# Operand spread with one transfer for both heads, and raw sums stored over 128 partitions, in attention with two dense layers

## Chip, cores and metric

One core of a Trainium2 chip. The metric is the device time of one execution in microseconds, the median of several runs. In the rows below PE is TensorE's matmul and PEld its weight load, DVE is VectorE, ACT is ScalarE, POOL is GpSimd, SP is SyncE; SPq is SyncE's queue, which issues nearly all DMA transfers of this kernel. "L537" is line 537 of the kernel before.

## What is computed

Attention with rotary positions for 4 batches of 8 heads (576 rows of 64), then two dense layers over the 2304 rows: one with a squared ReLU (512 to 2048 to 512), one with a gated SiLU (512 to 1536 to 512). All in float32.

```python
q_rot, k_rot = (rotate(q), rotate(k))
scores = scale * np.matmul(q_rot, k_rot.transpose(0, 1, 3, 2))
scores = scores - np.max(scores, axis=-1, keepdims=True)
attn = np.exp(scores)
attn = attn / (np.sum(attn, axis=-1, keepdims=True) + 1e-09)
attn_out = np.matmul(attn, v)
x = attn_out.transpose(0, 2, 1, 3).reshape(B * S, H * D)
r = np.maximum(x @ w_in, 0.0)
x = (s * (r * r) + b) @ w_out
g = x @ w_gate
out = (g * (1.0 / (1.0 + np.exp(-g))) * (x @ w_val)) @ w_out2
```

## The kernel before

Each float32 operand of a matmul is split into a high and a low part of the type that TensorE reads fast, and products are sums over the parts. The attention goes by pairs of heads, 16 pairs (NP). `prep(p)` loads q and k of a pair (L381), rotates them on GpSimd, transposes them on TensorE (L504) so that q stands in partitions 0 to 63 and k in 64 to 127, and splits the result: ScalarE writes the high part `hi` (tile `qkhi`, L513), VectorE the low part `lo` (`qklo`, L515), each 128 partitions by two heads of S = 576 columns. Both tiles have one buffer.

For pairs 2 to 15, ten transfers on SyncE's queue (L537, called a train in the prediction) then spread these parts over the operand tiles of the score matmuls: `a` (q: high part in the upper 64 partitions, low part in the lower, with 64 zero columns between the heads), `t` (k: low part above, high part below) and `kz` (k's high part above, zeros below). Each transfer has 64 partitions and one head. For pairs 0 and 1 the engines write the operands themselves (L523, L526). The operand tiles exist twice (z = p % 2), so the transfers of pair p overwrite what the scores of pair p - 2 read, and `hi` may be rewritten for pair p + 1 only when the transfers of pair p have read it.

`pair(p)` computes nine blocks of scores (L609), their maxima on VectorE (L612), the exponentials on ScalarE (L616), transposes them (L670, L673), splits them (L678, L685) and multiplies by v (L700, L702). The unnormalized sums of a pair go through `xr` (two buffers) to DRAM tiles `x_d`: for each head one store of the high half's sums (64 partitions) and one of the low half's (L721), so four stores a pair.

The dense layers run over five blocks of 512 or 384 rows. `x_load` brings a block from `x_d`, one transfer for each half (`xl`, `xh`) and batch piece, over 128 partitions (L750); GpSimd adds the halves (L778) and multiplies by reciprocals read from `r_d` (L766, L781), and the result is split. Block 0's load and conversion fall into the attention; each later block is loaded while the block before it is computed. The second layer reads its blocks from `y_d` by the same function.

The order of instructions on each engine is written out by a planner (`Schedule`): every operation has a priority and a reckoned duration, a transfer 0.55 us of SyncE, `size / 360e3` us of the DMA engines and 1.3 us to land. An engine runs its queue strictly in the written order, whatever is late. SyncE's queue also carries v (L433 to L437), q and k, the weights (L287, L289), `r_d` and the outputs. Transfers use eight completion slots in turn.

The lines of the spread and of the store:

```python
for s0, s1, d0 in a_pieces(0, 2 * S):
    n = s1 - s0
    ops.append(sp(a[0:64, d0:d0 + n], lambda s0=s0, s1=s1: st["hi"][0:64, s0:s1], s0 == 0))
    ops.append(sp(a[64:128, d0:d0 + n], lambda s0=s0, s1=s1: st["lo"][0:64, s0:s1]))
for s0 in (0, S):
    c = slice(s0, s0 + S)
    ops.append(sp(t[64:128, c], lambda c=c: st["hi"][64:128, c]))
    ops.append(sp(t[0:64, c], lambda c=c: st["lo"][64:128, c]))
    ops.append(sp(kz[0:64, c], lambda c=c: st["hi"][64:128, c]))
```

Of the kernel before, what the change touches and what calls it, by code (L numbers as in the profile page):

```python
# [8 lines left out]
F32 = mybir.dt.float32  # L9
F32R = mybir.dt.float32r  # L10
# [167 lines left out]
def tile_attention_moe_moe(  # L178
# [16 lines left out]
    nc = tc.nc  # L195
    B, H, S, D = q.shape
    NT, DM = out.shape
    KD = DM // 128
    F1 = w_in.shape[1] // 128
    F2 = w_gate.shape[1] // 128  # L200
    HS = S // 2
    NH = B * H
    NP = NH // 2
# [7 lines left out]
    LATE, LAST = 1 << 20, 1 << 21  # L211
# [5 lines left out]
    AVP = 30  # L217
# [4 lines left out]
    sch = Schedule()  # L222
# [7 lines left out]
    dram = ctx.enter_context(tc.tile_pool(name="dram", bufs=1, space=DRAM))  # L230
# [3 lines left out]
    late = {}  # L234
# [12 lines left out]
    at_c = att.enter_context(tc.tile_pool(name="at_c", bufs=1))  # L247
# [7 lines left out]

    x_d = [[dram.tile([DM, S], F32, name=f"x_d{half}{b}") for b in range(B)] for half in range(2)]
    r_d = [dram.tile([H // 2, 2 * S], F32, name=f"r_d{b}") for b in range(B)]
# [7 lines left out]
    a_t = [at_c.tile([128, 2 * S + 128], F32R, name=f"a{z}") for z in range(2)]  # L265
    t_t = [at_c.tile([128, 2 * S], F32R, name=f"t{z}") for z in range(2)]
    kz_t = [at_c.tile([128, 2 * S], F32R, name=f"kz{z}") for z in range(2)]

# [82 lines left out]
    up, dn = slice(0, 64), slice(64, 128)  # L351
# [3 lines left out]

    def a_pieces(c0, c1):

        if c0 < S:
            yield c0, min(c1, S), c0
        if c1 > S:  # L360
            yield max(c0, S), c1, max(c0, S) + 64

    def place(x, g, gap=0):

        c = S // G
        return x.rearrange("p (h s) -> p h s", h=2)[:, :, g * c:(g + 1) * c]
# [46 lines left out]
    def prep(p):  # L413
# [120 lines left out]
        if p > 1:  # L534
            def sp(o, i, first=False):
                return sch.dma(
                    256 * o.shape[1], lambda: nc.sync.dma_start(out=o.bitcast(F32), in_=i().bitcast(F32)), pr + 6, (*trs, *zeros[z]),  # L537
                    (tok,) if first else (), (hi_tok,), pace=1.3
                )
            ops = []  # L540
            for s0, s1, d0 in a_pieces(0, 2 * S):
                n = s1 - s0
                ops.append(sp(a[0:64, d0:d0 + n], lambda s0=s0, s1=s1: st["hi"][0:64, s0:s1], s0 == 0))
                ops.append(sp(a[64:128, d0:d0 + n], lambda s0=s0, s1=s1: st["lo"][0:64, s0:s1]))
            for s0 in (0, S):
                c = slice(s0, s0 + S)
                ops.append(sp(t[64:128, c], lambda c=c: st["hi"][64:128, c]))
                ops.append(sp(t[0:64, c], lambda c=c: st["lo"][64:128, c]))
                ops.append(sp(kz[0:64, c], lambda c=c: st["hi"][64:128, c]))
            for o in ops[1:]:  # L550
                ops[0].next.append(o)
                o.need += 1
# [24 lines left out]
    def pair(p, st):  # L577
# [10 lines left out]
        for u in range(NU):  # L588
# [3 lines left out]
            if u < QA:  # L592
                terms = ((128 * u, 0),)
            elif u == QA:
                terms = ((128 * u, 0), (128 * u + 64, S))
            else:
                terms = ((128 * u + 64, S),)

# [55 lines left out]
        def third(y, pr):  # L654
# [63 lines left out]
            j = y - 1  # L718
            for half in range(2):
                def put(half=half):  # L720
                    nc.sync.dma_start(out=x_d[half][b][128 * pp + 64 * j:128 * pp + 64 * j + 64], in_=st["xr"][64 * half:64 * half + 64, S * j:S * j + S])  # L721
                x_store[b].append(sch.dma(147456, put, pr + 25 + AVP, evs, (), (xr_tok,), pace=1.2))

# [15 lines left out]
    def x_load(st, pieces, n, prio, deps, pool_name, pool, batches=None):  # L739
# [4 lines left out]
        for z, (o, m, src) in enumerate(pieces):  # L744
            def ld(z=z, o=o, m=m, src=src):
                if z == 0:
                    st["xh"] = pool().tile([128, KD, 512], F32R, tag="xh", name="xh")[:, :, 0:n]
                    st["xl"] = pool().tile([128, KD, 512], F32R, tag="xl", name="xl")[:, :, 0:n]
                for name, part in zip(("xl", "xh"), src):
                    nc.sync.dma_start(out=st[name][:, :, o:o + m].bitcast(F32), in_=part.rearrange("(k p) t -> p k t", p=128))  # L750
            lds.append(sch.dma(len(src) * 2048 * m, ld, prio, deps, (xh_tok,) if z == 0 else (), after=lds[-1:]))
            lds[-1].dur = 0.55 * len(src)
# [164 lines left out]
    def block_b(i, j):  # L917
# [4 lines left out]
        for o, m, b, s in x_pieces(sum(UBS[:j]), UB, S):  # L922
            pieces.append((o, m, (x_d[0][b][:, s:s + m], x_d[1][b][:, s:s + m])))
            batches.append((b, s, m, o))
            deps += x_store[b]
# [31 lines left out]
    def block_2(i, j):  # L957
        st = {}
        UB = UBS[j]
        prio = LAST + 2000 * i  # L960
        outs, xh_tok = x_load(st, [(0, UB, (y_d[j],))], UB, prio - 1500 if i else LATE + 1000 * n_b, y_op[j], ("xhb", "xhc"), lambda: late[st["xh_tok"].pool])
        nt = UB // 128
# [64 lines left out]
        for c in range(nt):  # L1027
# [8 lines left out]
            for z in range(2):  # L1036
                b, g = divmod((sum(UBS[:j]) + c * 128) // 64 + z, PC)
                last = i == len(blocks) - 1 and z == 1
                def put(c=c, z=z, b=b, g=g, e=nc.scalar if last else nc.sync):
                    e.dma_start(out=out[b * S:(b + 1) * S].rearrange("(r g) m -> r g m", g=PC)[:, g], in_=st["y", c][64 * z:64 * z + 64])  # L1040
# [49 lines left out]
```

## Time and profile before

| | us |
|---|---|
| median of the runs shown | 1174.75 |
| lowest, highest of the runs | 1172.81, 3986.44 |
| profiled execution: time | 1175.48 |
| profiled execution: span | 1173.7 |

The span goes from the first to the last instruction of the profiled execution; the time of the same execution has 1.8 us more around it. Busy times are shares of the span; a matmul's end is modelled, so instructions of TensorE overlap in the rows, and a busy TensorE is not one at its peak. "PEclk" is the granted clock in parts of full speed. "DMA share" is the busy share of the 16 DMA engines, each packet counted for its whole time, so that it can pass 1. In a timeline the bracket behind an instruction gives the idle time of its engine before it and what ended it; a wait for several things is put down to the one that came last.

### The profile page before, as it was taken

What the parts mean: (1) busy time and instruction counts of PE and PEld (TensorE: products, weight loads), DVE (VectorE), ACT (ScalarE), POOL (GpSimd) and SP (SyncE); (2) the same over time, 40 slices, a digit from 0 to 9 for tenths busy, and PEclk for the clock granted to TensorE, in tenths of its full rate; (3) what the DMA queues carried; (4) which work ended last, traced back from release to release, by engine and by line L of the source; (5) the groups of instructions that cost most, each with busy time, mean ns of one, the idle gap of its engine ahead of it and who ended that gap; (6) DMA issues with size and microseconds to landing.
All of it is one profiled execution on the core that took longest, in us unless ns stands there. A gap on an engine that the chain in (4) does not pass through costs nothing.

```text
span 1173.7 us, 16604 instructions
## 1 busy us (share of the span) xinstructions
PE 1143.1 (97%) x6242; PEld 1009.1 (86%) x6242; DVE 616.2 (52%) x969; ACT 551.5 (47%) x1112; POOL 263.6 (22%) x222
## 2 busy tenths in 40 slices
PE   8989899999999999999999999999999999999998
PEld 7889888898887888888899998888888888899997
DVE  5879788999979943232242798811211211211111
ACT  4879888899877832232232566412111211211211
POOL 6776685743222031020020112200000000000000
PEclk8899999999999999999999999999999999999999
DMA  4588888767375640110110446301100200200100
GB/s 112 117 191 189 228 208 190 201 158 183 94 226 177 216 149 17 56 57 5 64 49 6 135 146 218 112 1 47 25 1 1 63 1 1 63 1 1 27 1 27
DMA packets 126335, 110.39 MB, mean 94 GB/s; under 512 B 68256, under 2 KB 103216, under 8 KB 126256
## 3 DMA queue, kind: packets, MB, share of 16 engines
q1 hardware_dynamic: 126016, 108.95, 34.3%
q8 instruction: 49, 0.80, 0.3%
q10 hardware_dynamic: 240, 0.39, 0.1%
q14 instruction: 30, 0.25, 0.1%
HBM read 69.71 MB, written 18.95 MB: 76 GB/s over the span
## 4 chain that ended last, share of the span: by engine, by line
PE 79%; DVE 8%; ACT 4%; DMA 3%; SPq 2%; issue 2%; POOL 1%; ACTq 0%; POOLq 0%; DVEq 0%
PE hb L798 14%; PE hb L800 14%; PE hb L799 14%; PE acc L799 5%; PE acc L800 5%; PE acc L798 5%; PE acc L983 4%; PE acc L985 4%; PE acc L984 4%; PE ps_s L609 3%; PE ps_t L670 2%; DVE nm L612 2%; SPq L537 2%; DVE pl L685 2%; PE ps_av L700 1%
## 5 line engine op out<-in xcount | busy, mean ns | idle before, releaser
L798 PE MATMUL hb<-xh,w 128*128 128x512 f32 (+1 forms) x800 | 296.3, 370 | 1.9 <-ACT w L331 1.4
L800 PE MATMUL hb<-xh,w 128*128 128x512 f32 (+1 forms) x800 | 296.0, 370 | 0.0
L799 PE MATMUL hb<-xl,w 128*128 128x512 f32 (+1 forms) x800 | 295.6, 370 | 0.0
L1013 DVE TENSOR_TENSOR si<-hb,si 128x512 f32<-128x512 f32 (+1 forms) x60 | 38.3, 638 | 276.4 <-PE hb L800 273.3
L798 PEld LDWEIGHTS hb<-xh,w 128*128 128x128 f32 x800 | 150.2, 188 | 23.8 <-ACT w L331 1.8
L800 PEld LDWEIGHTS hb<-xh,w 128*128 128x128 f32 x800 | 150.1, 188 | 21.0 <-DVE w L338 0.4
L799 PEld LDWEIGHTS hb<-xl,w 128*128 128x128 f32 x800 | 150.1, 188 | 21.0
L799 PE MATMUL acc<-gl,w 128*128 128x512 f32 (+1 forms) x320 | 118.2, 369 | 0.1
L1011 ACT ACTIVATE si<-hb 128x512 f32<-128x512 f32 (+1 forms) x60 | 33.3, 555 | 180.0 <-PE hb L800 174.3
L798 PE MATMUL acc<-gh,w 128*128 128x512 f32 (+1 forms) x320 | 117.9, 368 | 0.0
L800 PE MATMUL acc<-gh,w 128*128 128x512 f32 (+1 forms) x320 | 117.7, 368 | 0.0
L612 DVE TENSOR_REDUCE nm<-ps_s 128x1 f32<-128x576 f32 x144 | 108.3, 752 | 11.7 <-PE ps_s L609 10.4
L609 PE MATMUL ps_s<-t,a 128*128 128x288 f32 x320 | 103.6, 339 | 9.1 <-ACT e L616 7.4
L616 ACT ACTIVATE e<-ps_s,nm 128x576 f32<-128x576 f32 x144 | 107.1, 744 | 8.3 <-DVE nm L612 7.5
L678 ACT ACTIVATE ph<-ps_t 128x512 fp32r<-128x512 f32 x192 | 105.8, 570 | 9.6 <-PE ps_t L670 7.8
L1015 ACT ACTIVATE gh<-si 128x512 fp32r<-128x512 f32 (+1 forms) x60 | 35.4, 589 | 146.2 <-DVE si L1013 146.2
L850 DVE SCALAR_TENSOR_TENSOR r<-r,sv 128x512 f32<-128x512 f32 (+1 forms) x64 | 46.2, 722 | 108.0 <-ACT r L844 108.0
L700 PE MATMUL ps_av<-ph,vh 128*128 128x384 f32 (+1 forms) x320 | 97.8, 326 | 0.4 <-ACT xr L713 0.4
L844 ACT ACTIVATE r<-hb 128x512 f32<-128x512 f32 (+1 forms) x80 | 44.0, 551 | 114.9 <-PE hb L800 103.6
L685 DVE TENSOR_TENSOR pl<-ps_t,ph 128x512 fp32r<-128x512 f32 x144 | 96.0, 684 | 1.8 <-ACT ph L678 0.6
L670 PE MATMUL ps_t<-ident,e 128*128 128x128 f32 x576 | 88.4, 281 | 6.9 <-DVE qklo L515 4.3
L609 PE MATMUL ps_s<-kz,a 128*128 128x288 f32 x320 | 92.8, 305 | 0.1
(80 smaller groups left out, 1962.4 us busy)
## 6 DMA issues: line engine op xcount, KB each, us to landing
raw<-in_moe_w_out_dram SPq DMA_DIRECT2D x28, 512.0 KB, 3.6
x_d<-xr SPq DMA_DIRECT2D x64, 144.0 KB, 2.6
raw<-in_moe_w_in_dram SPq DMA_DIRECT2D x16, 512.0 KB, 3.9
raw<-in_moe_w_gate_dram SPq DMA_DIRECT2D x12, 512.0 KB, 3.5
raw<-in_moe_w_val_dram SPq DMA_DIRECT2D x12, 512.0 KB, 3.7
x<-in_q_dram SPq DMA_DIRECT2D x15, 288.0 KB, 3.6
x<-in_k_dram SPq DMA_DIRECT2D x15, 288.0 KB, 5.0
out_dram<-o SPq DMA_DIRECT2D x33, 128.0 KB, 2.4
```

Of the source, the lines that this page charges most:

```text
L609: nc.tensor.matmul(ps[:, hf * 512:hf * 512 + HS], a[:, q0:q0 + 128], m[:, k0:k0 + HS], start=y == 0, stop=y == len(todo) - 1)
L612: nc.vector.tensor_reduce(out=st["nm"][:, u:u + 1], in_=st["s", u], axis=AX.XY, op=ALU.max, negate=True)
L616: nc.scalar.activation(out=st["e", u].rearrange("p (f n) -> p f n", f=2), in_=st["s", u], func=AF.Exp, bias=st["nm"][:, u:u + 1], accum_ou ...
L670: nc.tensor.transpose(ps[:, z * 128:z * 128 + 128], st["e", u][:, kc * 128:kc * 128 + 128], ident)
L678: nc.scalar.activation(out=st["ph", y][0:rows, 512 * i:512 * i + n], in_=st["pt", y, i][0:rows, 0:n], func=AF.Copy)
L685: nc.vector.tensor_tensor(out=dst, in0=st["pt", y, i][0:rows, 0:n], in1=st["ph", y][0:rows, c].bitcast(F32), op=ALU.subtract)
L700: nc.tensor.matmul(ps, vv, st["ph", y][:, c], start=kc == 0, stop=kc == 4)
L798: nc.tensor.matmul(o, lh, rh, start=first, stop=False)
L799: nc.tensor.matmul(o, lh, rl, start=False, stop=False)
L800: nc.tensor.matmul(o, ll, rh, start=False, stop=last)
L983: nc.tensor.matmul(o, uh[:, cs], w[:, 0], start=first, stop=False)
L984: nc.tensor.matmul(o, uh[:, cs], w[:, 1], start=False, stop=False)
```

## The change

The tiles `t` and `kz` get 8 unused columns after each head (KS = S + 8), so that both heads of a destination can be addressed as one block with a gap, as in `a`. The ten transfers of a pair become five, each with both heads and twice the bytes. The two DRAM tiles of a batch for the halves become one, in which the two halves of a head stand one after the other, so that one store takes all 128 partitions. The load of a block has to gather the rows again: four transfers of 64 partitions for each piece instead of two of 128. The second head's scores read `t` and `kz` from column KS on.

```diff
--- before.py
+++ after.py
@@ -199,6 +199,7 @@
     F1 = w_in.shape[1] // 128
     F2 = w_gate.shape[1] // 128
     HS = S // 2
+    KS = S + 8
     NH = B * H
     NP = NH // 2
     PC = 2 * S // 128
@@ -253,7 +254,7 @@
     pl_p = att.enter_context(tc.tile_pool(name="pl", bufs=2))
     e_p = att.enter_context(tc.tile_pool(name="e", bufs=NE))
 
-    x_d = [[dram.tile([DM, S], F32, name=f"x_d{half}{b}") for b in range(B)] for half in range(2)]
+    x_d = [dram.tile([2 * DM, S], F32, name=f"x_d{b}") for b in range(B)]
     r_d = [dram.tile([H // 2, 2 * S], F32, name=f"r_d{b}") for b in range(B)]
     y_d = [dram.tile([DM, n], F32, name=f"y_d{j}") for j, n in enumerate(UBS)]
 
@@ -263,8 +264,8 @@
     rt = at_c.tile([128, PC, 3, D // 2], F32, name="rt")
     qs_t = at_c.tile([128, 1], F32, name="qs")
     a_t = [at_c.tile([128, 2 * S + 128], F32R, name=f"a{z}") for z in range(2)]
-    t_t = [at_c.tile([128, 2 * S], F32R, name=f"t{z}") for z in range(2)]
-    kz_t = [at_c.tile([128, 2 * S], F32R, name=f"kz{z}") for z in range(2)]
+    t_t = [at_c.tile([128, 2 * KS], F32R, name=f"t{z}") for z in range(2)]
+    kz_t = [at_c.tile([128, 2 * KS], F32R, name=f"kz{z}") for z in range(2)]
 
     def dma(o, i, size, prio, after=()):
         return sch.dma(size, lambda: nc.sync.dma_start(out=o, in_=i), prio, after=after)
@@ -353,14 +354,7 @@
     x_store = {b: [] for b in range(B)}
     spread_op = {}
 
-    def a_pieces(c0, c1):
-
-        if c0 < S:
-            yield c0, min(c1, S), c0
-        if c1 > S:
-            yield max(c0, S), c1, max(c0, S) + 64
-
-    def place(x, g, gap=0):
+    def place(x, g):
 
         c = S // G
         return x.rearrange("p (h s) -> p h s", h=2)[:, :, g * c:(g + 1) * c]
@@ -534,19 +528,15 @@
         if p > 1:
             def sp(o, i, first=False):
                 return sch.dma(
-                    256 * o.shape[1], lambda: nc.sync.dma_start(out=o.bitcast(F32), in_=i().bitcast(F32)), pr + 6, (*trs, *zeros[z]),
+                    512 * S, lambda: nc.sync.dma_start(out=o.bitcast(F32), in_=i().bitcast(F32)), pr + 6, (*trs, *zeros[z]),
                     (tok,) if first else (), (hi_tok,), pace=1.3
                 )
             ops = []
-            for s0, s1, d0 in a_pieces(0, 2 * S):
-                n = s1 - s0
-                ops.append(sp(a[0:64, d0:d0 + n], lambda s0=s0, s1=s1: st["hi"][0:64, s0:s1], s0 == 0))
-                ops.append(sp(a[64:128, d0:d0 + n], lambda s0=s0, s1=s1: st["lo"][0:64, s0:s1]))
-            for s0 in (0, S):
-                c = slice(s0, s0 + S)
-                ops.append(sp(t[64:128, c], lambda c=c: st["hi"][64:128, c]))
-                ops.append(sp(t[0:64, c], lambda c=c: st["lo"][64:128, c]))
-                ops.append(sp(kz[0:64, c], lambda c=c: st["hi"][64:128, c]))
+            def heads(x):
+                return x.rearrange("p (h s) -> p h s", h=2)[:, :, 0:S]
+
+            for dst, rows, name, src in ((a, up, "hi", up), (a, dn, "lo", up), (t, dn, "hi", dn), (t, up, "lo", dn), (kz, up, "hi", dn)):
+                ops.append(sp(heads(dst[rows]), lambda name=name, src=src: heads(st[name][src]), not ops))
             for o in ops[1:]:
                 ops[0].next.append(o)
                 o.need += 1
@@ -592,9 +582,9 @@
             if u < QA:
                 terms = ((128 * u, 0),)
             elif u == QA:
-                terms = ((128 * u, 0), (128 * u + 64, S))
+                terms = ((128 * u, 0), (128 * u + 64, KS))
             else:
-                terms = ((128 * u + 64, S),)
+                terms = ((128 * u + 64, KS),)
 
             def s_mm(u=u, terms=terms):
                 if u == 0:
@@ -716,10 +706,9 @@
             if y == 0:
                 return
             j = y - 1
-            for half in range(2):
-                def put(half=half):
-                    nc.sync.dma_start(out=x_d[half][b][128 * pp + 64 * j:128 * pp + 64 * j + 64], in_=st["xr"][64 * half:64 * half + 64, S * j:S * j + S])
-                x_store[b].append(sch.dma(147456, put, pr + 25 + AVP, evs, (), (xr_tok,), pace=1.2))
+            def put():
+                nc.sync.dma_start(out=x_d[b][256 * pp + 128 * j:256 * pp + 128 * j + 128], in_=st["xr"][:, S * j:S * j + S])
+            x_store[b].append(sch.dma(294912, put, pr + 25 + AVP, evs, (), (xr_tok,), pace=1.2))
 
         for y in range(3):
             third(y, base + TA + TB * y)
@@ -746,9 +735,9 @@
                 if z == 0:
                     st["xh"] = pool().tile([128, KD, 512], F32R, tag="xh", name="xh")[:, :, 0:n]
                     st["xl"] = pool().tile([128, KD, 512], F32R, tag="xl", name="xl")[:, :, 0:n]
-                for name, part in zip(("xl", "xh"), src):
-                    nc.sync.dma_start(out=st[name][:, :, o:o + m].bitcast(F32), in_=part.rearrange("(k p) t -> p k t", p=128))
-            lds.append(sch.dma(len(src) * 2048 * m, ld, prio, deps, (xh_tok,) if z == 0 else (), after=lds[-1:]))
+                for name, rows, part in src:
+                    nc.sync.dma_start(out=st[name][rows, :, o:o + m].bitcast(F32), in_=part)
+            lds.append(sch.dma((2 if batches else 1) * 2048 * m, ld, prio, deps, (xh_tok,) if z == 0 else (), after=lds[-1:]))
             lds[-1].dur = 0.55 * len(src)
         rbs, last = {}, lds[-1]
         half = n // 2
@@ -920,7 +909,8 @@
         prio = LATE + 1000 * i
         pieces, deps, batches = [], [], []
         for o, m, b, s in x_pieces(sum(UBS[:j]), UB, S):
-            pieces.append((o, m, (x_d[0][b][:, s:s + m], x_d[1][b][:, s:s + m])))
+            xv = x_d[b].rearrange("(k j f d) t -> f j d k t", j=2, f=2, d=64)
+            pieces.append((o, m, [(name, slice(64 * y, 64 * y + 64), xv[f, y][:, :, s:s + m]) for f, name in enumerate(("xl", "xh")) for y in range(2)]))
             batches.append((b, s, m, o))
             deps += x_store[b]
         outs, xh_tok = x_load(st, pieces, UB, prio - 800 if i else LATE - 900, deps, ("xhb", "xhc"), lambda: late[st["xh_tok"].pool], batches)
@@ -958,7 +948,7 @@
         st = {}
         UB = UBS[j]
         prio = LAST + 2000 * i
-        outs, xh_tok = x_load(st, [(0, UB, (y_d[j],))], UB, prio - 1500 if i else LATE + 1000 * n_b, y_op[j], ("xhb", "xhc"), lambda: late[st["xh_tok"].pool])
+        outs, xh_tok = x_load(st, [(0, UB, [("xl", slice(0, 128), y_d[j].rearrange("(k p) t -> p k t", p=128))])], UB, prio - 1500 if i else LATE + 1000 * n_b, y_op[j], ("xhb", "xhc"), lambda: late[st["xh_tok"].pool])
         nt = UB // 128
         a_toks = (Token("s"), Token("s"))
         acc_toks = (a_toks[0], a_toks[0], a_toks[1], a_toks[1])
```

## Rows read from the trace of the kernel before

**Rows 1.** Busy time by stretch: bounds, length, us busy (instructions), clock, DMA share, GB/s
```profile
60.00:240.00 180.00, 165.82 (x1257) 155.71 (x1256) 155.75 (x244) 150.80 (x358) 121.38 (x95) 0.99 0.83 201
240.00:320.00 80.00, 78.04 (x579) 71.91 (x579) 78.81 (x132) 73.49 (x171) 27.30 (x26) 1.00 0.55 137
320.00:1174.00 854.00, 846.33 (x4003) 732.07 (x4001) 339.66 (x523) 287.22 (x496) 74.09 (x67) 1.00 0.21 66
```
**Rows 2.** The same view in pieces of 5 us (PE, PEld, DVE, ACT, POOL)
```profile
70.00:75.00 5.00, 1.99 (x14) 1.93 (x15) 2.73 (x5) 3.34 (x9) 4.84 (x4) 1.00 0.57 135
...
135.00:140.00 5.00, 3.02 (x23) 2.67 (x21) 1.31 (x2) 0.44 (x2) 5.00 (x5) 1.00 0.88 211
140.00:145.00 5.00, 3.67 (x27) 3.23 (x28) 4.46 (x8) 5.00 (x13) 3.15 (x3) 1.00 0.95 214
...
155.00:160.00 5.00, 3.39 (x25) 2.99 (x23) 3.54 (x4) 2.05 (x6) 4.14 (x4) 1.00 0.89 237
...
195.00:200.00 5.00, 3.88 (x30) 3.36 (x28) 3.74 (x7) 3.64 (x9) 2.14 (x3) 1.00 0.76 196
```
**Rows 3.** Timeline of ScalarE, L513 after a train: start, us, instruction [idle before <-releaser]
```profile
71.66 0.58 ACT L513 ACTIVATE qkhi<-pst,qs 128x384 fp32r<-128x384 f32 x1 [3.22 <-DMA kz<-qkhi]
...
139.92 1.05 ACT L513 ACTIVATE qkhi<-pst,qs 128x384 fp32r<-128x384 f32 x2 [4.56 <-DMA kz<-qkhi]
...
157.62 0.58 ACT L513 ACTIVATE qkhi<-pst,qs 128x384 fp32r<-128x384 f32 x1 [1.98 <-PE ps_s L609]
...
196.36 1.05 ACT L513 ACTIVATE qkhi<-pst,qs 128x384 fp32r<-128x384 f32 x2 [2.02 <-DMA kz<-qkhi]
```
**Rows 4.** Timeline of SyncE's queue: start us, us, transfer issued
```profile
53.59 1.19 SPq L721 DMA_DIRECT2D x_d<-xr  x2
...
127.38 0.56 SPq L381 DMA_DIRECT2D x<-in_k_dram  x1
...
130.87 0.59 SPq L537 DMA_DIRECT2D a<-qkhi  x1
...
148.25 0.60 SPq L537 DMA_DIRECT2D a<-qkhi  x1
...
187.01 0.60 SPq L537 DMA_DIRECT2D a<-qkhi  x1
...
193.43 0.59 SPq L537 DMA_DIRECT2D kz<-qkhi  x1
```
**Rows 5.** Chain of work that ended last, in order of time: start, us, what
```profile
193.43 2.83 DMA kz<-qkhi
...
196.36 1.05 ACT qkhi L513 x2
```
**Rows 6.** Busy time in pieces of 1 us, columns as in rows 1
```profile
67.00:68.00 1.00, 1.00 (x11) 0.96 (x10) 1.00 (x3) 0.79 (x4) 1.00 (x1) 1.00 1.06 228
...
121.00:122.00 1.00, 1.00 (x11) 0.96 (x10) 1.00 (x2) 0.98 (x4) 0.00 (x0) 1.00 1.05 397
...
277.00:278.00 1.00, 1.00 (x11) 0.96 (x10) 0.97 (x2) 1.00 (x3) 0.00 (x0) 1.00 0.96 231
...
281.00:282.00 1.00, 1.00 (x9) 0.87 (x9) 1.00 (x2) 1.00 (x4) 1.00 (x1) 1.00 0.94 210
...
294.00:295.00 1.00, 1.00 (x11) 0.97 (x10) 1.00 (x2) 0.92 (x4) 0.00 (x0) 1.00 1.02 226
```
**Rows 7.** All 140 transfers of L537, from issue to landing
```profile
DMA to landing us min/median/max: 2.4/3.0/5.4
```
**Rows 8.** Timeline of TensorE, last score matmul of pairs 5 and 6
```profile
125.59 0.30 PE L609 MATMUL ps_s<-kz,a 128*128 128x288 f32 x1
...
145.74 0.29 PE L609 MATMUL ps_s<-kz,a 128*128 128x288 f32 x1
```
**Rows 9.** Waits of SyncE's queue: us in total, times, longest
```profile
SPq L381 <- DMA xh<-x_d: 4.2, 1, 4.2
```

## Prediction

> **What bounds the kernel now.** I read the busy time by stretch first, since a mean over the run hides the stages. From 320 us on, TensorE is busy 846.33 of 854 us: the two dense layers are bound by its matmuls, and no edit here takes a matmul away. In the attention, from 60 to 240 us, it is busy 165.82 of 180 us, so it idles 14.2 us; from 240 to 320 us it idles 2.0 us [rows 1]. That idle time is all that a better data path can win there. Before 60 us the pairs 0 and 1 go another way, without the transfers that are edited.
>
> Next I cut the stretch into pieces of 5 us to see where the 14.2 us lie [rows 2]: 3.0 us at 70 to 75, 2.0 and 1.3 at 135 to 145, 1.6 at 155 to 160, 1.1 at 195 to 200, and the rest in crumbs. Then the timeline of ScalarE at these places: each time the first `qkhi` activation (L513) of the next pair stood in front of its queue, with 3.22, 4.56, 1.98 and 2.02 us of idle time before it [rows 3]. `hi` has one buffer, so L513 may not overwrite it until the ten transfers of L537 have read it. The reader should see that these gaps are one wait, and that its length is set by when the last of the ten lands.
>
> What sets that landing? On SyncE's timeline the train for pair 10 starts at 187.01 and its last issue at 193.43 [rows 4]; the chain of waits shows that one landing after 2.83 us, at 196.26, and ScalarE starting at 196.36 [rows 5]. So 6.42 us go to nine steps of issue (0.71 each, one slow issue among them) and 2.83 to the last landing: 9.25 us in all.
>
> **What each edit costs, step by step.**
>
> *Ten spread transfers become five.* Five issues fewer at 0.71 are 3.6 us less of SyncE per pair, 14 pairs. For the landing I bound the gain from both sides. If only the issue limits, the train takes four steps of 0.71, the last landing of 2.83, and 0.64 us more for the doubled last transfer (147,456 bytes at 231 GB/s, the best rate of a train below [rows 6]): 6.3 us, 2.9 less. If the DMA engines limit, the bytes count, and they are the same: 1.475 MB. While trains run, the engines are busy 0.94 to 0.96 of the time at 210 to 231 GB/s, and where other loads had queued up before, 1.06 at 228 GB/s [rows 6]. At about 225 GB/s the data take 6.55 us. A single transfer lands in 2.4 us at the least [rows 7]; without its own 0.64 us of data that leaves 1.76. Sum 8.3 us, 0.95 less than 9.25. I take 1.0 us, near the engines' end: a share of 0.94 to 0.96 leaves almost nothing to fill, and a backlog did not make them faster. Both ends stay for the range.
>
> The rate has a second witness: the stores of raw sums, also of 64 partitions, moved 226 GB/s at a share of 1.02, while the load of block 0, of 128 partitions, moved 397 GB/s at 1.05 [rows 6]. [...]
>
> *When a train starts.* It overwrites operands that the scores two pairs earlier read. Pair 5's last score matmul starts at 125.59 and train 7 at 130.87; pair 6's at 145.74 and train 8 at 148.25 [rows 4, 8]: with 0.3 us for the matmul, 5.0 and 2.2 us in which SyncE was still issuing other things back to back. With 3.6 us less per train and two stores fewer of about 0.6 (two took 1.19 [rows 4]) that lag should go where it is only issue. Against it, the first merged transfer of a train now needs both heads' scores done, where the first two issues needed only the first head's; that is at most two steps, 1.3 us, and counts only where SyncE is early. The score matmuls of the new pair wait for both heads too, but train 8 lands near 157.6, at the L513 it holds up, and pair 8 is scored only after pair 7, whose scores follow pair 6's end at 146: ten microseconds and more of cover. If that cover went, the cost would be half a train, some 3 us.
>
> *Stores in one transfer of 128 partitions.* 64 issues become 32, about 0.6 us each, 1.2 us per pair; the data of two stores fall from 1.3 us (294,912 bytes at 226 GB/s) to 0.74 at 397. Nothing waits for them but the loads of a block and the buffer `xr`, of which there are two; their worth is only in SyncE's lag, counted above.
>
> *Loads of a block in quarters.* Each piece takes four issues of 64 partitions instead of two of 128, 1.2 us more. Block 0's is 2.1 MB and runs in the attention: 5.3 us at 397 GB/s, 9.3 us at 225, so 4.0 us more at most; nothing more if two quarters for opposite halves overlap in the engines. SyncE already stood 4.2 us for this load [rows 9], then issued the next load at 127.38 and train 7 at 130.87 [rows 4]. Issued some 3 us earlier by the shorter train before it, its end moves by about +1 us; I take no gain in the gap at 135 to 145. The other blocks are loaded beside the dense layers, where TensorE idles 7.7 us in 854, a buffer ahead: nothing.
>
> *The gap of 8 columns, the longer zeroing, the offset of the second head in the matmuls:* no instruction more, 16 of 1152 columns more in a memset of GpSimd. Nothing, bounded by 1.4% of it.
>
> *The planner's order.* It charges a transfer 0.55 us of SyncE and bytes times 1.3 over 360 GB/s. For the train that is 0.53 us of data per old transfer and 1.06 per new one, so the landing it reckons with hardly changes, and the order on TensorE, ScalarE and VectorE should mostly stay.
>
> **The sum.** Gap at 70: the train starts earlier by the two store issues saved (1.2) and lands 1.0 sooner: 2.2 of its 3.0. Gap at 135: 0. Gap at 155: 1.0 and the 2.2 of lag are more than its wait of 1.98, so all 1.6. Gap at 195: 1.1. Crumbs: 0.5. Together 5.4 us. The profiled execution took 1175.48 us (span 1173.7 and 1.8 around it), which is 0.7 above the median of 1174.75: 1175.5 - 5.4 = 1170.1, and I say 1170.
>
> **Rivals.**
> - *Issue was the limit after all.* For it: SyncE reached trains 7 and 8 late with nothing but other issues ahead, and a landing takes 3.0 us in the median, little above its least [rows 7], so transfers hardly queue. Against it: the shares of 0.94 to 1.06 [rows 6]. Then every landing is 2.9 us earlier, all 14.2 us go: 1161. [...]
> - *Nothing moves.* The wait is handed on: if L513 is no longer late, ScalarE and VectorE, busy 150.8 and 155.8 of 180 us [rows 1], set the pace in the same places, or the planner puts L513 earlier by as much. About 1175, two either way.
> - *Slower: block 0's quarters.* Place: 117 to 145 us. The load takes 4.0 us longer and SyncE, which stands for it, starts train 7 that much later; the gap at 135 grows from 3.3 to 7.3. Decides from the point where the other gaps give back less than 4.0 us. With none of them won: 1175.5 + 4.0 = 1179.5. For it: the 397 against 226 GB/s and the wait of 4.2. Against it: the load is issued earlier, and neighbouring quarters may overlap. [...]
>
> **How the numbers follow.** My forecast 0.48 (alone 1165 to 1173), issue-bound 0.17, nothing 0.20, slower 0.10, and 0.05 for an order of the planner that turns out quite different, by either sign. The range reaches from just below the issue-bound case to just above the slower one: 1160 to 1180; outside lie half of the last case and the far tails of the two ends, under 0.2. A time is told from no change only beyond about 2%, 23.5 us: 1151 or 1198. All idle time of the attention together is less than that, so faster has 0.03, slower 0.05 (the planner, or a load that stalls several trains), within 2% 0.92.
>
> **What would show it.** Right: 70 issues at L537 of twice the size, whose time to landing rises from 3.0 us to 4 or more; the first L513 after a train still starting at its landing, but with idle times before it about 1 to 2 us shorter; TensorE busy some 5 us more of an equal piece of the attention. The issue-bound rival is right if trains move 280 GB/s or more. The block's load in quarters is seen in GB/s after the train of pair 6: near 225 or near 400. Wrong would be the forecast if TensorE waits for a spread transfer directly, or if the dense layers change in length.

## The result, and the profile after

The changed kernel takes 1181.63 us in the median of 5 runs (1178.72 to 1183.06), beside 1172.81 for the kernel before in runs on the same chip. The ratio is 1.0074, interval 1.0053 to 1.0096: 0.7% slower, by 8.7 us. The forecast was 1170 and 1160 to 1180. All ratios below compare medians of many executions; the rows come from one profiled execution each (span 1181.3 us here), and single executions scatter by some 3 us. Differences under that are not read from rows alone.

Busy time by stretch of the changed kernel, columns as in [rows 1]:

```profile
60.00:240.00 180.00, 163.38 (x1230) 154.08 (x1229) 155.73 (x243) 148.29 (x352) 120.96 (x93) 0.98 0.83 197
240.00:320.00 80.00, 76.25 (x576) 70.89 (x575) 76.50 (x128) 72.66 (x172) 28.18 (x27) 1.00 0.52 134
320.00:1174.00 854.00, 849.90 (x4028) 734.80 (x4027) 340.54 (x527) 289.10 (x499) 73.94 (x66) 1.00 0.23 66
```
Against [rows 1] TensorE is busy 2.4 us less from 60 to 240 us, where it was to be 5 us more, and it gets through 27 matmuls fewer there. In the last stretch it is busier than before (849.90 against 846.33): it is still working where the kernel before was done. The pieces that answer to [rows 2], the same columns:

```profile
135.00:140.00 5.00, 4.91 (x38) 4.49 (x36) 4.10 (x6) 3.18 (x7) 3.99 (x5) 1.00 0.93 244
140.00:145.00 5.00, 0.00 (x0) 0.00 (x0) 0.40 (x1) 1.01 (x2) 2.42 (x2) 1.00 0.80 203
145.00:150.00 5.00, 4.66 (x24) 4.42 (x25) 3.30 (x7) 4.41 (x12) 4.32 (x5) 0.66 0.49 119
...
160.00:165.00 5.00, 2.06 (x16) 1.64 (x15) 2.22 (x4) 2.83 (x7) 4.53 (x4) 1.00 1.12 266
```
One hole stands out. From 140 to 145 us TensorE does nothing, and in the next piece its granted clock is 0.66 on average: by pieces of 1 us it is 0.53, 0.50, 0.50 and 0.77 from 145 to 149 us and 1.00 after that, and the piece holds 24 matmuls in 4.66 us where the one at 1.00 from 135 to 140 held 38 in 4.91. The timeline of ScalarE, as [rows 3] (L507 is L513 of before), shows what stands at the hole:

```profile
68.75 0.58 ACT L507 ACTIVATE qkhi<-pst,qs 128x384 fp32r<-128x384 f32 x1 [1.51 <-PE ps_s L599]
...
143.99 0.58 ACT L507 ACTIVATE qkhi<-pst,qs 128x384 fp32r<-128x384 f32 x1 [5.49 <-DMA kz<-qkhi]
...
162.17 1.05 ACT L507 ACTIVATE qkhi<-pst,qs 128x384 fp32r<-128x384 f32 x2 [3.75 <-DMA kz<-qkhi]
```
The gap at 70 shrank (3.22 to 1.51); the two after it grew (4.56 to 5.49, 1.98 to 3.75). SyncE's timeline says why for the longest, as [rows 4]; L739 loads block 0, L375 the next pair's k, L429 its v, L531 is train 6 at 107.11 and train 7 at 134.43:

```profile
107.11 0.64 SPq L531 DMA_DIRECT2D a<-qkhi  x1
...
113.87 4.48 SPq L739 DMA_DIRECT2D xl<-x_d  x2
118.40 1.96 SPq L739 DMA_DIRECT2D xh<-x_d  x2
...
121.76 2.52 SPq L375 DMA_DIRECT2D x<-in_k_dram  x1
124.33 4.70 SPq L429 DMA_DIRECT2D vr<-in_v_dram  x1
...
134.43 0.63 SPq L531 DMA_DIRECT2D a<-qkhi  x1
```
The issues of the four quarters take 6.4 us, the one of v stands 4.70 us while the load ahead of it is still being moved (its last quarter lands at 128.3), and train 7 starts at 134.43: 8.7 us after pair 5's scores are done (125.7), against 5.0 before. In the kernel before, train 6 and the same load are issued at

```profile
110.01 0.59 SPq L537 DMA_DIRECT2D a<-qkhi  x1
...
116.44 0.59 SPq L750 DMA_DIRECT2D xl<-x_d  x1
```
so the load follows its train by 6.4 us there and by 6.8 us in the changed kernel. Train 8, at the third gap, was not followed further: it starts at 150.39 and lands 11.7 us later.

The landing of the 70 spread transfers, as [rows 7], and the waits of ScalarE for the train (us in total, times, longest):

```profile
DMA to landing us min/median/max: 3.3/5.5/8.5
...
ACT qkhi L507 <- DMA kz<-qkhi: 17.9, 8, 5.5
```
For the kernel before, the same wait reads

```profile
ACT qkhi L513 <- DMA kz<-qkhi: 11.0, 4, 4.6
```

### The profile page after: what moved, and what is told of

It reads as the page before. It is cut to its first block, busy times and chain, and to the rows that moved or that the text cites. A ratio compares the mean times of both kernels' runs of the same rounds, so it can differ in the third digit from the quotient of the medians.

```text
span 1181.3 us, 16504 instructions
## 1 busy us (share of the span) xinstructions
PE 1143.1 (97%) x6242; PEld 1008.7 (85%) x6242; DVE 615.2 (52%) x969; ACT 551.2 (47%) x1112; POOL 264.2 (22%) x222
## 4 chain that ended last, share of the span: by engine, by line
PE 73%; DVE 10%; DMA 7%; ACT 5%; SPq 3%; issue 2%; ACTq 0%; POOL 0%; DVEq 0%; POOLq 0%
PE hb L787 13%; PE hb L789 13%; PE hb L788 13%; DMA kz<-qkhi 5%; PE acc L788 5%; PE acc L789 4%; PE acc L787 4%; PE acc L975 4%; PE acc L973 4%; PE acc L974 4%; PE ps_s L599 3%; SPq L531 2%; DVE nm L602 2%; DVE pl L675 2%; PE ps_t L660 2%
```

## The experiments

Kernels called "old order" keep the instruction order of the four compute engines exactly as in the kernel before: the planner was given the old costs, so that only the transfers differ.

**Merged spread alone, old order.** Ten transfers planned, five issued.

```
-  a[0:64, ...] <- hi, a[64:128, ...] <- lo, t <- hi, t <- lo, kz <- hi   (for each head)
+  dma_start(out=heads(dst[rows]), in_=heads(st[name][src]))               (both heads, 5 transfers)
```


> Only the spread is merged (five transfers of both heads, with the gap), and the planner still sees ten, so TensorE, VectorE, ScalarE and GpSimd run the order of the kernel before, instruction for instruction; stores and loads of the raw sums are as before. Theory 'load' (the quartered load of block 0 is what costs): 5 us or so faster than before, since SyncE has 70 issues fewer. Theory 'train' (a merged transfer runs slower, because it keeps all engines on one half of the partitions for twice as long): 0 to 6 us slower, with trains that land 0.5 to 1 us later than the 9.0 us of before. Theory 'order' (the planner's new order costs): no slower than before, within 3 us.

1.0010 [0.9992, 1.0027]: nothing that is clear of the noise. Train 7 of this kernel: SyncE's timeline, the activation behind it, a piece of 1 us in an earlier train, and the landing of all 70:

```profile
128.41 0.63 SPq L546 DMA_DIRECT2D a<-qkhi  x1
...
130.71 1.49 SPq L546 DMA_DIRECT2D t<-qklo  x1
132.25 1.38 SPq L546 DMA_DIRECT2D kz<-qkhi  x1
133.66 1.60 SPq L727 DMA_DIRECT2D x_d<-xr  x1
```
```profile
138.66 1.05 ACT L514 ACTIVATE qkhi<-pst,qs 128x384 fp32r<-128x384 f32 x2 [5.08 <-DMA kz<-qkhi]
```
```profile
66.00:67.00 1.00, 1.00 (x10) 1.00 (x9) 0.94 (x3) 0.60 (x1) 1.00 (x2) 1.00 0.97 207
```
```profile
DMA to landing us min/median/max: 3.4/5.3/7.0
```
The last issue goes out 3.8 us after the first (6.2 in the same train with ten), so the issue did get shorter, although single issues now take 1.4 to 1.5 us where they took 0.6. The rate stays at 207 GB/s with the engines busy 0.97. And the train still lands 10 us after its first issue, at 138.5. Over the six trains whose last landing the trace holds (pairs 6, 7, 9, 10, 12, 13) that is 10.2 us on average; for the four of them whose last landing the trace of before holds too (6, 7, 9, 13) it is 10.3, against 9.2 before. What the five saved issues bring forward is the next transfers on the queue (here the store at 133.66): from 1.5 us after the first issue to the landing, the engines moved 1.82 MB on average in these six trains, 1.58 before, and 0.24 MB at 225 GB/s is 1.1 us. So in the extra time the engines did not stand still, they worked on other transfers. That these are the reason is argued and not shown: a train that landed late for a reason of its own would let as many bytes pass, and no run holds the followers back. Set against the kernel before matmul by matmul, this execution is 3.3 us ahead when its first train starts and 1.5 behind at the 1500th matmul; what it loses along its trains is more than the medians show, and is one execution's.

**Merged spread alone, the planner told.** The same edit with the changed kernel's costs.

> The spread alone is merged, and the planner knows it: its order differs from the kernel before in some 250 places on VectorE and 290 on ScalarE. Theory 'load': as the same edit in the old order, about 5 us faster. Theory 'train': 0 to 6 us slower. Theory 'order': 5 to 9 us slower, while the same edit in the old order is not.

1.0041 [1.0025, 1.0057]. The transfers are those of the run above, so the 0.3% (3.6 us) between the two is the order of work, SyncE's queue included. By position, 285 of VectorE's 969 instructions differ from the kernel before, 418 of ScalarE's 1112 and 1005 of TensorE's 6242 matmuls.

**Store in one transfer and loads in quarters, with the new order and with the old.**

```
-  x_d[half][b][...] <- xr[64*half:64*half+64]    (two transfers)     xl, xh <- 128 partitions
+  x_d[b][256*pp+128*j : +128] <- xr              (one transfer)      xl, xh <- up, dn of 64 partitions
```


> The raw sums alone are changed, and the planner knows it: its order differs from the kernel before in some 260 places on VectorE and on ScalarE. Theory 'load': 4 to 8 us slower, as in the old order. Theory 'train': within 2 us. Theory 'order': 5 to 9 us slower, while the same edit in the old order is not.

> Only the raw sums are changed (one store of 128 partitions, loads of a block in quarters of 64), and the planner is told the old issue times, so the engines run the order of the kernel before. Theory 'load': 4 to 8 us slower, with the TensorE gap at 135 to 145 us grown from 3.3 to 5 us or more, and train 7 that starts 9 us after the scores it waits for instead of 5. Theory 'train': within 2 us of before, or faster. Theory 'order': within 3 us of before.

1.0039 [1.0019, 1.0058] and 1.0049 [1.0028, 1.0071]: slower by the same amount in either order. So the loss of this half of the change is in its transfers, and here the new order costs nothing.

**The two halves of it apart.** First the loads alone in quarters, from the old tiles; then the store alone, with loads of 128 partitions in the order of the store. The second leaves out the regrouping of the rows, so it adds other numbers together; its transfers and their sizes are those of a whole computation.

```
-  for name, part in zip(("xl", "xh"), src): dma_start(out=st[name][:, :, o:o+m], in_=part)
+      for rows in (up, dn): dma_start(out=st[name][rows, :, o:o+m], in_=part[rows])
```


> The kernel before with one edit: a block is loaded from the old two tiles in four transfers of 64 partitions instead of two of 128; order of the engines as before. Theory 'load' (quarters move at 226 GB/s instead of some 350, and what is queued behind them, train 7 in the attention and the raw weights behind block 1's load, comes late): 5 to 8 us slower, with the TensorE gap near 140 us at 5 us or more and a new one near 345 us of 2 us, and a granted clock of half speed behind each. Rival 'store' (the merged store or the new layout in DRAM costs): within 2 us of before.

> The raw sums stored in one transfer of 128 partitions, and the blocks loaded in two transfers of 128 partitions that take the rows as the store left them, so the heads' halves are added in the wrong pairs: the regrouping of the rows is left out, all sizes and the order of the engines are as before. Theory 'load': the whole cost of the edit is gone, so 0 to 4 us faster than before by 32 issues and the faster stores. Rival 'store': 4 to 6 us slower, as with the quarters.

Quarters 1.0098 [1.0076, 1.0121], 11.5 us slower; the store 0.9971 [0.9951, 0.9991], 3.4 us faster. Apart they make 0.69%, together 0.39 to 0.49%; the intervals leave room for that. With the store, the idle time before the first `qkhi` of each pair adds up to 13.9 us instead of 17.6 (gap at 70: 1.2 instead of 3.22), while the mean from a train's first issue to the last landing that the trace holds stays at 9.0: trains start earlier, they do not run faster.

**The quarters by block.** Block 0's load in quarters, then all but block 0's (a condition on the block in the diff above).

> Kernel before with only the load of the first block of the dense part (the one that runs inside the attention) in quarters of 64 partitions; the other blocks' loads whole, order of work as before. All blocks in quarters cost a ratio of 1.0098 (+12 us). Theory 'each load pays': this one load costs the 4 us that were seen between 115 and 143 us and nothing after 320 us: ratio 1.0035. Theory 'the first load decides': the later delays (at 345, 427, 600 us) are only its shift handed on, so that they come here too: ratio 1.010. Theory 'the first delay is swallowed by the slack at the end of the attention': 1.000.

> The complement of the run with only the first block in quarters: here the first block's load is whole and the later ones are in quarters, order of work as before. All together cost 1.0098, the first alone 1.0031. Theory 'each load pays its own': 1.006 to 1.008, TensorE's idle time all after 330 us, in front of it waits of ScalarE's weight split for raw weights behind the load. Theory 'the two go together' (the later loads only hurt because the first shifted them): 1.002 or less.

1.0031 [1.0017, 1.0045] and 1.0073 [1.0058, 1.0089]; together 1.0104, inside the interval of the 1.0098. Each part pays its own. Block 0's, in a piece of 1 us, and what follows on ScalarE and in pieces of 5 us:

```profile
121.00:122.00 1.00, 1.00 (x10) 1.00 (x9) 1.00 (x3) 1.00 (x3) 0.00 (x0) 1.00 1.09 199
```
```profile
141.61 1.05 ACT L513 ACTIVATE qkhi<-pst,qs 128x384 fp32r<-128x384 f32 x2 [8.51 <-DMA x_d<-xr]
```
```profile
135.00:140.00 5.00, 0.76 (x5) 0.44 (x3) 0.00 (x0) 0.00 (x0) 5.00 (x5) 0.78 0.90 216
140.00:145.00 5.00, 2.10 (x10) 2.10 (x11) 2.59 (x5) 3.13 (x7) 4.03 (x3) 0.50 0.83 188
```
The same microsecond moved 397 GB/s before, at about the same share of the engines, 1.05 [rows 6]. Half the rate, a gap of 8.51 instead of 4.56, and the clock at 0.50 after it. (The bracket names a store that L513 does not need; the train's last transfer, issued at 138.34, lands at 141.35.) The four quarters of a piece go alternately to the upper and the lower 64 partitions, back to back in the queue, and still move 199 GB/s: two halves side by side did not add up here.

The later blocks: pieces of 5 us, SyncE and ScalarE, of the kernel with only these in quarters:

```profile
335.00:340.00 5.00, 5.00 (x23) 4.14 (x23) 3.60 (x6) 3.58 (x7) 0.00 (x0) 1.00 1.06 210
340.00:345.00 5.00, 5.00 (x23) 4.13 (x23) 0.69 (x1) 0.45 (x1) 0.97 (x1) 1.00 1.11 246
345.00:350.00 5.00, 3.64 (x15) 2.44 (x13) 3.40 (x6) 4.21 (x7) 2.44 (x3) 1.00 0.79 227
350.00:355.00 5.00, 4.30 (x12) 3.48 (x13) 4.97 (x9) 3.72 (x7) 1.13 (x1) 0.67 0.52 177
```
```profile
329.23 1.30 SPq L751 DMA_DIRECT2D xl<-x_d  x2
...
333.89 1.28 SPq L751 DMA_DIRECT2D xh<-x_d  x2
...
336.63 0.52 SPq L289 DMA_DIRECT2D raw<-in_moe_w_in_dram  x1
```
```profile
345.63 0.66 ACT L302 ACTIVATE dec<-raw 128x512 f32<-128x512 f32 x1 [5.18 <-DMA raw<-in_moe_w_in_dram]
```
and of the kernel before, the same load and the same activation:

```profile
335.00:340.00 5.00, 5.00 (x24) 4.13 (x23) 2.86 (x4) 3.48 (x6) 2.12 (x2) 1.00 1.03 336
340.00:345.00 5.00, 5.00 (x24) 4.14 (x23) 4.03 (x6) 3.94 (x7) 1.75 (x2) 1.00 0.49 135
345.00:350.00 5.00, 5.00 (x24) 4.14 (x23) 4.83 (x8) 3.49 (x7) 0.91 (x1) 1.00 0.53 178
```
```profile
339.62 0.67 ACT L302 ACTIVATE dec<-raw 128x512 f32<-128x512 f32 x1 [1.03 <-DMA raw<-in_moe_w_in_dram]
```
TensorE does not wait for the block itself, which is a buffer ahead. But a tile of raw weights stands behind it in the same queue, and its consumer has no such lead. It starts at 345.63 instead of 339.62 (1.9 of the 6.0 us are an earlier shift: the load's first issue is at 329.23 here and at 327.36 before), after 5.18 us of idle time instead of 1.03; ScalarE and VectorE, which split the weights into two parts, fall idle (0.45 and 0.69 us busy from 340 to 345), and a few microseconds later TensorE does (3.64 us busy from 345 to 350), with a granted clock of 0.67 after it. The same matmul (the 2400th) starts 4.2 us later against the kernel before than the 2300th did. Some 1.2 us of it are given back; further steps of 0.5 to 1.7 us follow, near 428, 520, 600 and 730 us, and were not traced one by one.

**The changed kernel with its loads whole.** Its own order, merged spread and gap stay; the loads take the rows in the order of the store, and the regrouping is left out again.

```
-  xv = x_d[b].rearrange("(k j f d) t -> f j d k t", ...)   four quarters
+  xv = x_d[b].rearrange("(k j p) t -> j p k t", p=128)     two transfers of 128 partitions
```


> Changed kernel with its store as it is (128 rows to one place), but each block loaded in two transfers of 128 partitions in the order in which it was stored; the regrouping of the rows for the two halves is left out, so other numbers are added; merged spread, gap and the changed order of work stay. Theory 'the quarters are the loss': of the changed kernel's 1.0074 about 1% goes, and it comes to 0.997 to 1.001. Theory 'the order is the loss': about 1.004 stays. Theory 'the merged spread is the loss' (its slower issue delays other loads): 1.004 too, with trains that still land after 9.6 us.

1.0008 [0.9994, 1.0021]. The 0.7% is gone. Its rows around the hole (pieces of 5 us, SyncE, ScalarE):

```profile
135.00:140.00 5.00, 2.62 (x22) 2.34 (x19) 2.54 (x5) 2.40 (x7) 2.18 (x3) 1.00 0.75 194
140.00:145.00 5.00, 4.89 (x24) 4.66 (x25) 3.13 (x6) 4.25 (x11) 4.46 (x4) 0.66 0.60 128
```
```profile
128.59 0.63 SPq L531 DMA_DIRECT2D a<-qkhi  x1
```
```profile
138.76 0.58 ACT L507 ACTIVATE qkhi<-pst,qs 128x384 fp32r<-128x384 f32 x1 [2.55 <-DMA kz<-qkhi]
```
Pair 5's scores end at 123.4 here, so train 7 is 5.2 us late instead of 8.7, and the gap 2.55 instead of 5.49. The two kernels run the same matmuls in the same order, so they can be set against each other matmul by matmul: of the 10.6 us between these two executions, 2.3 are there before block 0's load (scatter from the start of the run), 6.3 come from that load to the end of the attention, 2.8 in the dense layers, and 0.8 are given back.

**Other orders and the gap.** The ten old transfers with `a` and `t` alternating, so that neighbours read and write opposite halves of the partitions; and the gap of 8 columns alone.

```
-  a hi, a lo, a hi, a lo, t hi, t lo, kz, t hi, t lo, kz
+  a hi 0, t hi 0, a hi 1, t hi 1, a lo 0, t lo 0, a lo 1, t lo 1, kz 0, kz 1
```


> The ten spread transfers of before, unmerged, in another order among themselves: neighbours read from and write to opposite halves of the partitions (a high, t high, a low, t low, head by head, kz last). Order of the compute engines as before. Theory 'halves' (a train is limited by the half of the partitions that all engines work on, and neighbours on opposite halves overlap): trains land in 7.0 to 8.3 us instead of 9.0, and the kernel is 3 to 8 us faster. Rival 'step' (all engines work through a queue in step, so halves don't overlap): trains of 9.0, within 2 us.

> Only the gap of 8 columns in t and kz, with ten transfers in the old sequence; the second head's rows then start 32 bytes off. Theories 'load' and 'order': within 2 us of before, trains that land in 9.0 us. Rival 'gap' (the shifted rows are what slows the spread): 3 us slower or more, trains of 9.5 us.

0.9979 [0.9966, 0.9992] and 1.0005 [0.9991, 1.0019]. The gap costs nothing that is clear of the noise. The alternating order gains 2.5 us, but not by overlap: a train takes 9.1 us on average (9.0 before). The idle time before `qkhi` falls from 17.6 to 13.7 us, and trains begin a little earlier (train 7 at 129.23 instead of 130.87). Why they do stays open.

**One store of 128 partitions without the quarters.** To keep the loads whole, the store may write its two halves to two places:

```
-  x_d[0][b], x_d[1][b] <- two transfers of 64 partitions
+  x_d[b].rearrange("(f r) s -> f r s", f=2)[:, r:r+64] <- xr[:, ...]     one transfer
```


> Kernel before with the store in one transfer of 128 partitions that writes the two halves 512 rows apart, the loads of a block whole as before, ten spread transfers, order of work as before; the whole computation is done. Theory 'store': the same gain as the run in which the regrouping was left out (0.9971), so 0.996 to 0.998. Theory 'the scattered write costs': a store whose 128 rows go to two places is slower than one to one place, and the gain is gone: 1.000.

> The kernel of the store in one transfer with whole loads, and the ten spread transfers in the alternating order (a, t, a, t, ... kz last). Alone the two gave 0.9971 and 0.9979. Theory 'two gains': 0.995. Theory 'one wait': both shorten the same idle time before the first qkhi activation after a train, and together they give no more than the larger alone: 0.997.

The same store in the changed kernel:

> Changed kernel with one part undone: the store of 128 partitions writes its two halves 512 rows apart, so that a block is loaded again in two transfers of 128 partitions; the merged spread, the gap and the changed order of work stay as in the changed kernel. Theory 'the quarters are the loss': the changed kernel's 1.0074 loses about 1% and comes to 0.998 to 1.000. Theory 'the order is the loss': it stays near 1.004, the ratio of the merged spread with its own order. If nothing changes (1.007), the quarters are no cause in this company.

1.0794 [1.0763, 1.0826], 1.0690 [1.0666, 1.0713] and 1.0800 [1.0777, 1.0822]: every theory missed by far. In the first of them, a microsecond in which nothing but such a store is moved, the last issue of a train that stands behind another (x_d at 157.44, the train from 158.03 on), and the wait for that train:

```profile
98.00:99.00 1.00, 1.00 (x6) 1.00 (x6) 1.00 (x2) 0.75 (x3) 0.00 (x0) 0.50 0.13 51
```
```profile
168.21 0.60 SPq L537 DMA_DIRECT2D kz<-qkhi  x1
```
```profile
171.30 1.05 ACT L513 ACTIVATE qkhi<-pst,qs 128x384 fp32r<-128x384 f32 x2 [11.43 <-DMA x_d<-xr]
```
The bracket names a store again, one issued at 170.31; what L513 needs are the readers of `hi`, and the last of these, issued at 168.21, lands at 171.23 by the counts of its completion slot. A share of 0.13 is what 2 of the 16 engines give when they are always busy, and 51 GB/s moved at it. The destination's leading dimension is 2; that this is the cause is the author's reading, and the run below whose store leads with 128 agrees with it (0.9964 where this one has 1.0794). What these runs say of the quarters is hidden under it. The way out is a layout in which both sides lead with 128: the rows of the two heads of a pair alternate in `x_d`, the store writes every second row, a block loads 128 adjacent rows, and the rows of the first layer's weights are loaded in the same order:

```
+  x_d[b].rearrange("(k p j) s -> k j p s", p=128, j=2)[pp, j] <- xr       store
+  xl, xh <- x_d[b].rearrange("(k f p) t -> f p k t", f=2, p=128)[f]       loads, whole
+  raw[j::2] <- w_in rows of head j                                        weights, two transfers
+  rbx <- both heads' reciprocals, alternating                             one transfer, two before
```


> Kernel before with the store in one transfer of 128 partitions in which the 128 rows stand evenly spaced (the rows of the two heads of a pair alternate), so that a block is loaded whole, in two transfers of 128 partitions; the rows of the first layer's weights are loaded in the same alternating order, in two transfers over every second partition, and a reciprocal's broadcast becomes one transfer instead of two; ten spread transfers, order of work as before. Theory 'two places': the 8% of the scattered store came from its leading dimension of 2, not from the distance of the rows: then this gives the gain of the run without regrouping, 0.995 to 0.998. Theory 'spacing': a store whose rows are not adjacent is slow in itself: 1.05 or more. If every second partition loads as slowly as 64 neighbours, the weights of the first layer come later and the dense layers pay: 1.000 to 1.005.

> The same with the ten spread transfers in the alternating order. Theory 'two gains': about 0.995, the fastest of all. Theory 'one wait': both gains shorten the same idle time before the first qkhi activation, and it stays at 0.997.

0.9964 [0.9947, 0.9980], and with the alternating order 0.9945 [0.9928, 0.9962]: 1168.0 us against 1175.4, the fastest here, ahead of both kernels. The two gains add up. The first of the two runs has 32 issues fewer on SyncE's queue than the store alone (504 against 536, the halved reciprocals included), so how much of its gain is the store's is not separated; the changed kernel with this layout was not run. In the faster one the idle time before the first `qkhi` of each pair adds up to 12.6 us instead of 17.6. Its first stretch, and its wait at train 7, 4.22 us against 4.56 before [rows 3]:

```profile
60.00:240.00 180.00, 170.13 (x1307) 160.34 (x1307) 160.68 (x256) 156.60 (x372) 130.53 (x100) 1.00 0.80 206
```
```profile
134.00 1.05 ACT L516 ACTIVATE qkhi<-pst,qs 128x384 fp32r<-128x384 f32 x2 [4.22 <-DMA rbx<-r_d]
```
Here too the bracket names a neighbour: the train's last transfer lands at 133.89.

## Why the prediction was wrong, step by step

The step that failed is the price of the loads in quarters. The sum puts it at nothing: the gap at 135 stays as it is, and the other blocks cost nothing. In the changed kernel it is 0.66%, 7.8 us (1.0074 against 1.0008 with the loads whole); the two profiled executions differ by 8.3 us from block 0's load on, 6.3 in the attention and 2.8 in the dense layers, with 0.8 given back. Two smaller steps failed beside it: the order of work, put at nothing, costs 3.6 us, and the 1.0 us per merged train is not there. Only the store gave what it was to give, and more.

- **Where the time can be won** (14.2 us of idle time in the attention, set by the landing of trains): right in the main. Three of the four rows name a transfer of the train; the one at 157.62 names a score matmul [rows 3], so that this gap is the train's is not shown. The attention is also where most of the time was lost.
- **A train lands 1.0 us sooner:** wrong; in the old order it lands 1.0 us later. That the engines and not the issue set the landing was right (1.0010, 207 GB/s at 0.97), and the issue rival fell with its 2.9 us per train. The sum of 8.3 us gave the engines to the train alone; that they are shared with what follows in the queue, which a shorter issue lets in sooner, is the likely reason and is not shown. The sign named for it came half: the median landing rose from 3.0 to 5.5 us, but the idle times did not shrink.
- **The start of a train, and the store:** right in kind. The store over 128 partitions is worth 3.4 us by itself, through earlier starts as far as the gaps show; the sum credited it with 1.2 at one gap and a part of the lag at another. But the issues saved on the spread added nothing to it.
- **Block 0's load in quarters, up to +4.0 us, +1 taken, gap at 135 unchanged:** the dearest step. Alone, in the old order, the load costs 3.6 us, just inside the bound; in the changed kernel the attention loses 6.3, which is over it. The reason given for the low end, an earlier issue through a shorter train, did not hold: counted from the first issue of the train before it, the load is issued after 6.8 us, 6.4 before, and its own issues then stand in SyncE's way for 6.4 us.
- **The other blocks, "a buffer ahead: nothing":** wrong, and in the old order the dearer part: 0.73%, 8.6 us. The lead of the load's own buffer was looked at, and not what is queued behind the load, as had been done for train 7. "If the dense layers change in length" was named as a sign of a wrong forecast, and it came. In the changed kernel's order the dense layers lose less, 2.8 us by the comparison. There a tile of weights is issued between the two pieces of block 1's load (at 337.09), and the longest wait for raw weights around it is 3.9 us instead of 5.2; that this is the whole reason was not tested.
- **"The order should mostly stay":** wrong, and worth 0.3%, 3.6 us. Costs that "hardly change" were enough to move hundreds of instructions.
- **The gap of 8 columns:** right, 1.0005.
- **The rivals:** the slower one (block 0's quarters, 1179.5) was the right mechanism, with a chance of only 0.10. The order had a chance of 0.05, by either sign; the later blocks' loads had no rival of their own.

Put together from the runs: merged spread with its order +0.41%, store -0.29%, quarters +0.66%, in sum 0.78% for the 0.74% measured. Since the last term is read from the changed kernel itself, the test lies in the other two: 0.41 and -0.29 make 0.12, and the changed kernel with its loads whole measured 0.08. The 0.98% of the quarters in the old order does not carry over whole; in the changed kernel they cost a third less.

## What to carry to other kernels

When a transfer is made slower, price it by what stands behind it in its queue, not by how early its own data are wanted: here, in the old order, loads with a buffer to spare cost 8.6 us, and the one that was traced did so through the weights behind it. Merging transfers shortened the issue and won nothing where the engines were already busy at 0.94 and more. And whoever trades one layout for another should look at both ends: a store over 128 partitions was worth 0.3%, the loads that it split cost twice that, and a layout that keeps both whole was there.

## What the runs showed of the hardware that was not expected

- A store whose destination leads with a dimension of 2 moved 51 GB/s at a share of 0.13, what 2 of the 16 engines give when they are always busy. What stood behind such stores in the queue waited: ScalarE 11.43 us for one train.
- Merged transfers took longer to issue: 1.4 to 1.5 us each at the end of a train, 0.6 for half the size. The first two of a merged train took 0.6 as well (0.64 and 0.61 in train 6 of the changed kernel), so it looks as if the issue is held back once transfers are queued; no run tests that.
- Every second partition was not like 64 neighbours here, 366 against 199 GB/s. In the run with alternating rows, a microsecond in which nearly all that moves are the weights of `raw[j::2]`, two transfers one behind the other, each over every second partition (356 packets of 1024 bytes):

```profile
265.00:266.00 1.00, 1.00 (x11) 1.00 (x9) 1.00 (x2) 1.00 (x4) 0.00 (x0) 1.00 1.05 366
```
Quarters of 64 neighbours, alternately of the upper and the lower half, moved 199 GB/s at 1.09. By packets: those of 2048 bytes of block 0's load took 85 to 102 ns over 128 partitions and 153 to 177 in quarters, on average over pieces of 1 us. So here 366 GB/s were moved without a transfer over all 128 partitions; the two transfers of every second partition were not timed apart.
